# One block schedule for a fused state-space and ReGLU kernel: halved first steps, G moved to the output stage, the C split by one VectorE op

## The chip, the cores and the metric

The kernel runs on one core of a Trainium2 chip. The metric is the device time of one execution in microseconds (us); several executions are timed and the median is given. A profiled execution also has a *span*, from its first to its last instruction; in the profiled runs here the time is 1.6 to 1.8 us longer than the span.

Engines in the profile: PE is TensorE (matmuls), PEld its weight loads, DVE is VectorE, ACT is ScalarE, POOL is GpSimd, SP issues most DMAs. "L442" is a line of that kernel's own source, so the same statement has another number in another kernel.

## The reference

Batch 4, 8 heads, 768 tokens, head size 32, state size 16; then 3072 tokens through a ReGLU feed-forward of 256 to 1536 to 256.

```python
# state-space part, per chunk of tokens (cut)
cum = np.cumsum(log_a, axis=-1)
M = (C @ B.T) * exp(cum_i - cum_j) * causal
y = M @ x + (C @ state) * exp(cum)
state = decay_full * state + sum_j B_j x_j * decay_from_j
# feed-forward
gate = np.maximum(x @ w_gate, 0.0)
val = x @ w_val
out = (gate * val) @ w_out
```

## The kernel before

The kernel works in chunks of 128 tokens. Two chunks are a *pair* (256 tokens, 12 pairs), two pairs are a *block* of the feed-forward (512 tokens, 6 blocks). For a pair, TensorE *turns* B and C (transposes), computes *G* (C times B) into four PSUM banks, the running *state* (A_ps), *inter* (C times state) and *D* (masked G times x). D and inter accumulate in one bank `y`, which is copied to `yT`, the input of the feed-forward. While block b runs, the attention of block b+1 is slipped between its matmuls. ScalarE and VectorE keep to the order of the program even where a later instruction is ready first: in the timeline of block 3 below, a relu whose gate was ready about 100.7 us starts at 102.44, behind a split of C that waited 1.51 us, and VectorE's BT copy, whose turn was done about 100.3, starts at 101.39, behind two others. The kernel uses eight PSUM banks: five are shared by everything (gate, val, G, outputs), and `tp`, `y` and `A_ps` have their own.

The parts that matter here:

```python
def tevac(p, beng, ceng, ceng1=None):       # evacuate a turn: BT, and C split by head parity
    ...
    put(beng, BT, 0, None)                  # inside blocks: beng = VectorE
    for t in range(2):
        put(ceng1 or ceng if t else ceng, CT[:, :, t], 1, t)   # inside blocks: ScalarE, two ops

def gevac(p, q, on_act, meng=None):         # mask one of the four banks of G
    if on_act:
        nc.scalar.copy(out=dst, in_=src)
        (meng or nc.gpsimd).tensor_tensor(out=dst, in0=dst, in1=m, op=ALU.mult)
    else:
        nc.vector.tensor_tensor(out=dst, in0=src, in1=m, op=ALU.mult)

def gv(b, f):                               # one gate/value step, 512 tokens wide, two banks
    g, v = bank("gate"), bank("val")
    ... 2 + 2 matmuls of 512 columns ...
    nc.scalar.activation(r, g, AF.Relu)
    nc.vector.tensor_tensor(out=fst[b][:, f], in0=r, in1=v, op=ALU.mult)   # h

# ... [cut] the prologue does all attention of pairs 0 and 1, then:
for b in range(NBLK):
    for f in range(NF):                     # 12 gate/value steps
        gv(b, f)
        # ... [cut] blocks 0, 1 and 2 on have three different placements.
        # Blocks 0 and 1 hold G and D of a pair here; all hold turns, states, scales.
    fout(b, 0); G(Q); gevacs(Q, ...)        # [cut] blocks 2 on
    fout(b, 1); foevac(b, 1); fout(b, 2)
    G(R); gevacs(R, ...)                    # a pair of the block after next
    Dm(Q); yevac(Q, nc.scalar)
    fout(b, 3); foevac(b, 3)
```

## Time and profile before

| | before |
|---|---|
| median of the three executions | 151.74 us |
| span of the profiled execution | 148.8 us |
| PE / DVE / ACT / POOL busy | 89 / 58 / 53 / 32 % |
| block 0's first gate matmul | 20.1 us |

The busy table of the page gives, per engine, busy us, share of the span and number of instructions:

```profile
PE 131.8 (89%) x1048; PEld 74.8 (50%) x1060; DVE 86.6 (58%) x171; ACT 78.8 (53%) x152; POOL 47.4 (32%) x72
```

TensorE bounds the kernel, but the busy times of its matmuls overlap (379 ns on average for 512 columns, while such matmuls start 216 ns apart), so 89% doesn't say how much is lost. The better measure is the length of each block against its own work. TensorE's timeline gives the first gate matmul of every block; cut there, the windows view of the kernel before reads as follows (stretch, length, then busy us and instructions per engine, granted TensorE clock, DMA share, GB/s). The rows are the prologue, blocks 0 to 5 and the tail:

```profile
0.00:20.12 20.12, 15.68 (x115) 7.74 (x117) 13.43 (x44) 7.20 (x16) 11.96 (x26) 1.00 1.18 170
20.12:45.22 25.10, 22.78 (x198) 13.55 (x199) 14.62 (x27) 13.82 (x30) 9.29 (x13) 1.00 0.73 99
45.22:70.51 25.29, 21.33 (x173) 11.82 (x176) 14.08 (x25) 14.31 (x28) 8.22 (x11) 1.00 0.44 64
70.51:90.63 20.12, 19.23 (x162) 10.94 (x163) 12.76 (x23) 12.07 (x23) 6.89 (x10) 1.00 0.55 79
90.63:110.74 20.11, 19.11 (x160) 10.81 (x161) 12.47 (x22) 12.02 (x23) 6.89 (x10) 1.00 0.56 80
110.74:128.86 18.12, 17.97 (x150) 10.70 (x151) 10.99 (x19) 10.56 (x19) 4.19 (x6) 1.00 0.09 30
128.86:144.66 15.80, 15.71 (x97) 9.24 (x95) 8.26 (x12) 8.24 (x14) 0.00 (x0) 1.00 0.10 34
144.66:148.80 4.14, 0.00 (x0) 0.00 (x0) 0.00 (x0) 0.59 (x1) 0.00 (x0) 0.79 0.18 63
```

A block's feed-forward alone is 48 matmuls of 512 columns, 0.216 us apart, and 48 of 256 columns, 0.109 us apart: 15.6 us. Block 5, which carries nothing else, takes 15.8. Two pairs of attention add about 2.6 us (my estimate, from the distances between their matmuls in the same timeline: 1.3 a pair, itemised in the prediction), so blocks 1 to 4 could take about 18.2 us. Blocks 1, 2 and 3 take 25.3, 20.1 and 20.1.

The waits view of the kernel before (who waited for whom; us in total, times, longest) shows some of it:

```profile
ACT CT L331 <- DVE BT L329: 11.7, 10, 1.5
PE y L410 <- POOL gs L359: 2.6, 4, 0.9
PE o L456 <- DVE h L449: 1.6, 3, 0.8
PE val L445 <- ACT r L448: 1.2, 3, 0.5
```

PE's own entries are small. The largest line is an engine off the critical path, ScalarE, standing still for VectorE before it splits C. How this reaches TensorE is seen in the timeline around one turn in block 3 of the kernel before (start, length, engine, line, op, out<-in, idle before and releaser; rows between those shown are left out):

```profile
99.91 0.40 PE L314 MATMUL tp<-ident,bs 128*128 128x128 bf16 x4
100.14 0.59 PE L442 MATMUL gate<-yT,wg 128*128 128x512 bf16 x2
100.47 0.42 DVE L380 TENSOR_TENSOR Sm<-A_ps,smask 128x256 bf16<-128x256 f32 x1
100.80 0.68 DVE L449 TENSOR_TENSOR h<-r,val 128x512 bf16<-128x512 bf16 x1
101.39 0.28 DVE L329 COPY BT<-tp 128x256 bf16<-128x256 bf16 x1
101.71 0.84 ACT L331 ACTIVATE CT<-tp,tmask 128x256 bf16<-128x256 bf16 x2 [1.51 <-DVE BT L329]
102.44 1.57 ACT L448 ACTIVATE r<-gate 128x512 bf16<-128x512 f32 x3
103.09 0.59 PE L445 MATMUL val<-yT,wv 128*128 128x512 bf16 x2 [0.41 <-ACT r L448]
105.35 0.28 PE L456 MATMUL o<-wo,h 128*128 128x256 bf16 x1 [0.41 <-DVE h L449]
```

The turn is done about 100.3 us. ScalarE's next instruction is the C split, but it waits for VectorE's BT copy, which reads the same `tp`, and that copy stands behind a state copy and an h in VectorE's own queue (from 100.47 to 101.39 us). ScalarE idles 1.51 us, then splits C for 0.84 us, and only then do three relus follow in one burst, the first of which had its gate ready about 100.7 us. The value matmul at 103.09 and the last output matmul at 105.35 pay for it.

### The profile page before, as it was taken

The numbers are of one execution on the slowest core, as the hardware profiler recorded it, in microseconds if no ns is written. First come the engines' busy times: TensorE is split into PE (matmuls) and PEld (weight loads), VectorE is DVE, ScalarE is ACT, GpSimd is POOL, SyncE is SP. The second block draws the span as 40 slices with busy tenths as digits, with TensorE's granted clock in tenths as the row PEclk, the third lists the DMA queues.
The fourth block names the chain that finished last, engine by engine and source line by source line (L and its number), as shares of the span: only waits on it lengthen the run. The fifth ranks groups of instructions, "written<-read, shape, count | busy, mean of one in ns | idle before, by whom it ended". The sixth has DMA issues, their size and how long they took to land. (4 is left out here: it accounts for less than half of the span.)

```text
span 148.8 us, 2882 instructions
## 1 busy us (share of the span) xinstructions
PE 131.8 (89%) x1048; PEld 74.8 (50%) x1060; DVE 86.6 (58%) x171; ACT 78.8 (53%) x152; POOL 47.4 (32%) x72
## 2 busy tenths in 40 slices
PE   6969689977998995779999899998899999999980
PEld 2445335444773443357454476444664447644670
DVE  5369857848154592545666555756738587088500
ACT  3124633676536663446766538766266673467320
POOL 6069530408277055014704038140245003000000
PEclk9999999999999999999999999999999999999997
DMA  4999999994023975002699012995012000120011
GB/s 99 180 162 184 214 202 196 119 119 39 4 73 92 121 98 49 0 0 75 119 105 125 4 44 93 130 121 49 0 71 73 4 0 0 71 75 0 0 71 71
DMA packets 68942, 12.08 MB, mean 81 GB/s; under 512 B 62720, under 2 KB 68928, under 8 KB 68928
## 3 DMA queue, kind: packets, MB, share of 16 engines
q1 hardware_dynamic: 63664, 9.02, 40.2%
q0 software_dynamic: 3184, 2.36, 10.4%
q10 hardware_dynamic: 2080, 0.52, 2.2%
q8 instruction: 8, 0.13, 0.4%
q14 instruction: 6, 0.05, 0.2%
HBM read 11.11 MB, written 3.15 MB: 96 GB/s over the span
## 5 line engine op out<-in xcount | busy, mean ns | idle before, releaser
L449 DVE TENSOR_TENSOR h<-r,val 128x512 bf16<-128x512 bf16 x72 | 48.6, 686 | 34.7 <-ACT r L448 25.8
L448 ACT ACTIVATE r<-gate 128x512 bf16<-128x512 f32 x72 | 41.9, 601 | 11.4 <-PE gate L442 11.2
L442 PE MATMUL gate<-yT,wg 128*128 128x512 bf16 x139 | 42.1, 379 | 1.7 <-DVE yT L422 0.9
L445 PE MATMUL val<-yT,wv 128*128 128x512 bf16 x138 | 41.5, 379 | 1.6 <-ACT r L448 1.2
L456 PE MATMUL o<-wo,h 128*128 128x256 bf16 x288 | 34.8, 273 | 1.6 <-DVE h L449 1.6
L359 POOL TENSOR_TENSOR gs<-gs,maskUT 128x512 bf16<-128x512 bf16 x18 | 20.5, 1155 | 48.8 <-ACT gs L358 36.2
L456 PEld LDWEIGHTS <-h 128*128 128x128 bf16 x288 | 27.3, 98 | 7.9 <-DVE h L449 2.4
L445 PEld LDWEIGHTS <-wv 128*128 128x128 bf16 x144 | 14.0, 97 | 19.4 <-issue 3.2
L331 ACT ACTIVATE CT<-tp,tmask 128x256 bf16<-128x256 bf16 x22 | 9.3, 471 | 18.9 <-DVE BT L329 11.7
L442 PEld LDWEIGHTS <-wg 128*128 128x128 bf16 x144 | 13.0, 97 | 12.0 <-issue 2.3
L260 POOL TENSOR_TENSOR bs<-bcr,scaleBC 128x256 bf16<-128x256 f32 x16 | 9.6, 623 | 16.6 <-DMA bcr<-in_C_dram 11.5
L463 ACT COPY ob<-o 128x512 f32<-128x512 f32 x12 | 7.0, 587 | 8.6 <-PE o L456 8.3
L380 DVE TENSOR_TENSOR Sm<-A_ps,smask 128x256 bf16<-128x256 f32 x20 | 8.4, 418 | 0.6 <-PE A_ps L372 0.5
L159 PE MATMUL w<-warm 128*128 128x512 bf16 x17 | 7.3, 570 | 1.3 <-DVE xr L90 1.2
L428 ACT CAST yT<-y 128x512 bf16<-128x512 f32 x9 | 5.3, 592 | 4.8 <-PE y L410 4.8
L392 PE MATMUL y<-CT,Sm 128*128 128x128 bf16 x40 | 6.2, 220 | 1.4 <-ACT CT L331 0.6
L392 PEld LDWEIGHTS <-Sm 128*128 128x128 bf16 x40 | 3.6, 97 | 6.0 <-issue 1.3
L314 PEld LDWEIGHTS <-bs 128*128 128x128 bf16 x48 | 3.6, 103 | 4.8 <-DVE bs L260 2.0
L314 PE MATMUL tp<-ident,bs 128*128 128x128 bf16 x44 | 4.7, 227 | 1.3 <-DVE bs L260 1.1
L410 PE MATMUL y<-gs,xb 128*32 128x128 bf16 x128 | 3.7, 222 | 1.7 <-POOL gs L359 1.6
L279 POOL CAST xb<-xr 128x512 bf16<-128x512 f32 x8 | 4.9, 612 | 0.0
L260 POOL TENSOR_TENSOR bs<-bcr,wf_422 128x256 bf16<-128x256 f32 x4 | 2.4, 618 | 7.4 <-DVE wf_422 L217 7.4
(167 smaller groups left out, 123.6 us busy)
## 6 DMA issues: line engine op xcount, KB each, us to landing
out_dram<-ob SPq DMA_DIRECT2D x12, 256.0 KB, 2.1
xr<-in_x_dram SPq DMA_DIRECT2D x16, 128.0 KB, 3.6
bcr<-in_B_dram SPq DMA_DIRECT2D x16, 64.0 KB, 3.6
bcr<-in_C_dram SPq DMA_DIRECT2D x16, 64.0 KB, 3.3
wg<-in_moe_w_gate_dram POOLq DMA_DIRECT2D x3, 256.0 KB, 6.3
wv<-in_moe_w_val_dram POOLq DMA_DIRECT2D x3, 256.0 KB, 7.2
wo<-in_moe_w_out_dram POOLq DMA_DIRECT2D x1, 768.0 KB, 9.9
xr<-in_x_dram ACTq DMA_DIRECT2D x2, 256.0 KB, 4.7
```

Of the source, the lines that this page charges most:

```text
L159: nc.tensor.matmul(out=w, lhsT=warm[:, 0:128], rhs=warm, start=True, stop=True)
L260: eng.tensor_tensor(out=bs.rearrange("s k (q t n) -> s k t q n", q=4, t=2)[:, :, t], in0=src[:, :, t], in1=f[:, :, 4 * t:4 * t + 4].to_bro ...
L314: nc.tensor.transpose(out=s["tp"][k][:, i], in_=s["tin"][k][i], identity=ident)
L331: eng.mul(dst, src, tmask[:, t:t + 1])
L359: (meng or nc.gpsimd).tensor_tensor(out=dst, in0=dst, in1=m, op=ALU.mult)
L380: nc.vector.tensor_tensor(out=carry["S"], in0=A_ps, in1=smask, op=ALU.mult)
L392: nc.tensor.matmul(out=s["y"][:, t, i], lhsT=Sm[:, t], rhs=s["CT"][:, i, t], start=not s["open"], stop=False, skip_group_check=True)
L442: nc.tensor.matmul(out=g, lhsT=wg[:, k, fs], rhs=yT[:, k, tk], start=(k == 0), stop=(k == 1))
L445: nc.tensor.matmul(out=v, lhsT=wv[:, k, fs], rhs=yT[:, k, tk], start=(k == 0), stop=(k == 1))
L448: nc.scalar.activation(r, g, AF.Relu)
L449: nc.vector.tensor_tensor(out=fst[b][:, f], in0=r, in1=v, op=ALU.mult)
L456: nc.tensor.matmul(out=o[:, ts % 2], lhsT=fst[b][:, f, ts * 128:(ts + 1) * 128], rhs=wo[:, f], start=(f == 0), stop=(f == NF - 1), skip_gr ...
```

## The change

The intent is one schedule for all blocks:

- The first three gate/value steps of a block (four in block 0) are done in two halves of 256 tokens. The first halves need only the first pair's yT; inter and D of the block's second pair (W) run behind the second first-half (third in block 0), and the second halves come after W's yT copy.
- No G among the gate/value steps. All G stand in the output stage.
- A turn inside a block is evacuated by ScalarE (BT) and VectorE (C, both parities in one op) for the block's first pair P, and by ScalarE alone for its second pair Q (in block 0, Q's turn stands in the output stage and is split like P's). The order in CT becomes parity first.
- G's masks: ScalarE copies 1.5 banks and GpSimd applies `affine_select`; VectorE multiplies 2.5 banks by the mask.
- The prologue starts block 0 after pair 0's yT; pair 1's sort, state, inter and D move into block 0. Two more dummy matmuls keep TensorE busy at the start. The last block's outputs leave in 128-row pieces.

The core of the diff (cut):

```diff
-    put(beng, BT, 0, None)
-    for t in range(2):
-        put(ceng1 or ceng if t else ceng, CT[:, :, t], 1, t)
+    (beng.copy if beng is nc.scalar else beng.tensor_copy)(rows(BT), tokens(0))
+    if ceng is nc.scalar:
+        for t in range(2):
+            nc.scalar.mul(rows(CT[:, t]), tokens(1), tmask[:, t:t + 1])
+        return
+    nc.vector.tensor_tensor(out=out_, in0=src.to_broadcast(shape),
+                            in1=mk.to_broadcast(shape), op=ALU.mult)
 ... [cut] gevac, keep_warm 8 -> 9 and 4 -> 5, prologue, tail
+        nh = 4 if b == 0 else 3
+        for f in range(nh):
+            gvh(b, f, 0)
+            if f == nh - 2:
+                inter(W, 0)
+                inter(W, 1)
+                Dm(W)
+                yevac(W, nc.scalar)
+        for f in range(nh):
+            gvh(b, f, 1)
+        for f in range(nh, NF):
+            gv(b, f)
+            if at("turn P", 8, 6, 5):
+                turn(P)
+                tevac(P, nc.scalar, nc.vector)
+            if at("state P0", 10, 8, 7):
+                state(P, 0)
+            if at("state P1", 11, 10, 9):
+                state(P, 1)
+            if at("turn Q", 99, 9, 8):
+                turn(Q)
+                tevac(Q, nc.scalar, nc.scalar)
+        fout(b, 0)
+        if more:
+            G(P)
+            gevac(P)
+        fout(b, 1)
+        state(Q, 0)
+        fout(b, 2)
+        if more:
+            inter(P, 0); inter(P, 1); Dm(P); yevac(P, nc.scalar)
+            G(Q); gevac(Q); state(Q, 1)
+        fout(b, 3)
```

(Some lines are joined or left out, among them block 0's own. `at(name, x, y, z)` is true after step x in block 0, y in block 1, z in the later blocks.)

More of the change, by code (lines that the diff above doesn't have):

```diff
@@ L123 @@
     nc.vector.memset(warm, 0.0)
+    wide_x(0, nc.scalar, nc.vector)
+    wide_x(1, nc.scalar, nc.vector)
     identf = const.tile([2 * BH, 2 * BH], FP32)
@@ L129 @@
     make_upper_triangular(nc, maskUT[:, 0], 1.0, diag=True)
-    wide_x(0, nc.scalar, nc.vector)
-    wide_x(1, nc.scalar, nc.vector)
     zero1 = const.tile([2 * BH, 1], FP32)
@@ L159, in keep_warm @@
             nc.tensor.matmul(out=w, lhsT=warm[:, 0:128], rhs=warm, start=True, stop=True)
-    keep_warm(8)
+    keep_warm(9)
     wg = glob.tile([128, 2, DF], BF16)
@@ L314, in transp, with tevac @@
             nc.tensor.transpose(out=s["tp"][k][:, i], in_=s["tin"][k][i], identity=ident)
-    def tevac(p, beng, ceng, ceng1=None):
+    def tevac(p, beng, ceng):
         s = st[p]
@@ L321, in tevac, with tokens, rows @@
         s["CT"] = CT = att.tile([128, 2, 2, 128], BF16, tag="CT", name="CT")
-        def put(eng, dst, k, t):
+        wide = p < NWIDE
+        def tokens(k, lead=""):
             src = tp[k]
-            if p < NWIDE:
-                dst = dst.rearrange("s c (m r) -> s c m r", r=2)
-                src = src.rearrange("s r (c m) -> s c m r", c=2)
-            if t is None:
-                (eng.copy if eng is nc.scalar else eng.tensor_copy)(dst, src)
-            elif eng is nc.scalar:
-                eng.mul(dst, src, tmask[:, t:t + 1])
-            else:
-                eng.tensor_scalar_mul(dst, src, tmask[:, t:t + 1])
-        put(beng, BT, 0, None)
-        for t in range(2):
-            put(ceng1 or ceng if t else ceng, CT[:, :, t], 1, t)
+            if wide:
+                return src.rearrange("s r m -> s m r")
+            return src.rearrange("s i m -> s (i m)")
+        def rows(dst):
+            dst = dst.rearrange("s i m -> s (i m)")
+            return dst.rearrange("s (m r) -> s m r", r=2) if wide else dst
+        (beng.copy if beng is nc.scalar else beng.tensor_copy)(rows(BT), tokens(0))
[3 more added lines that the diff above has]
+            return
+        src = tokens(1).unsqueeze(1)
+        out_ = CT.rearrange("s t i m -> s t (i m)")
+        if wide:
+            shape = [128, 2, 128, 2]
+            out_ = out_.rearrange("s t (m r) -> s t m r", r=2)
+            mk = tmask.unsqueeze(2).unsqueeze(3)
+        else:
+            shape = [128, 2, 256]
+            mk = tmask.unsqueeze(2)
+        nc.vector.tensor_tensor(out=out_, in0=src.to_broadcast(shape),
+                                in1=mk.to_broadcast(shape), op=ALU.mult)
     def G(p):
@@ L345, in G @@
                 nc.tensor.matmul(
-                    out=g[q][:, i], lhsT=s["BT"][r, i], rhs=s["CT"][r, i],
+                    out=g[q][:, i], lhsT=s["BT"][r, i], rhs=s["CT"][r, :, i],
                     start=(i == 0), stop=True, tile_position=(32 * q, 0),
@@ L350, in G, with causal, gevac, sevac @@
         s["gs"] = att.tile([128, 4, 4, 128], BF16, tag="gs", name="gs", bufs=2)
-    def gevac(p, q, on_act, meng=None):
+    def causal(dst, n):
+        nc.gpsimd.affine_select(
+            out=dst, in_=dst, pattern=[[0, n], [1, 128]], compare_op=ALU.is_ge,
+            fill=0.0, base=0, channel_multiplier=-1)
+    def gevac(p):
         s = st[p]
-        src = s["gp"][q].rearrange("j i t m -> j (i t) m")
-        dst = s["gs"][:, q]
+        g = [t.rearrange("j i t m -> j (i t) m") for t in s["gp"]]
+        d = s["gs"]
         m = maskUT.to_broadcast([128, 4, 128])
-        if on_act:
-            nc.scalar.copy(out=dst, in_=src)
-            (meng or nc.gpsimd).tensor_tensor(out=dst, in0=dst, in1=m, op=ALU.mult)
-        else:
-            nc.vector.tensor_tensor(out=dst, in0=src, in1=m, op=ALU.mult)
-    carry = {}
+        nc.scalar.copy(out=d[:, 0], in_=g[0])
+        causal(d[:, 0], 4)
+        nc.scalar.copy(out=d[:, 1, 2:4], in_=g[1][:, 2:4])
+        causal(d[:, 1, 2:4], 2)
+        for q in (2, 3):
+            nc.vector.tensor_tensor(out=d[:, q], in0=g[q], in1=m, op=ALU.mult)
+        nc.vector.tensor_tensor(out=d[:, 1, 0:2], in0=g[1][:, 0:2], in1=m[:, 0:2],
+                                op=ALU.mult)
+    S = {}
     def astep(p, i):
         c = 2 * (p % PPB) + i
-        s = st[p]
         if c == NC - 1:
-            carry.pop("S", None)
             return
         nc.tensor.matmul(
-            out=A_ps, lhsT=s["B"][i], rhs=s["x"][i],
+            out=A_ps, lhsT=st[p]["B"][i], rhs=st[p]["x"][i],
             start=(c == 0), stop=(c == NC - 2), skip_group_check=True)
-        carry["next"] = att.tile([128, 2, 128], BF16, tag="Sm", name="Sm")
-    def sevac():
-        if "next" in carry:
-            carry["S"] = carry.pop("next")
-            nc.vector.tensor_tensor(out=carry["S"], in0=A_ps, in1=smask, op=ALU.mult)
-    def inter(p, i):
-        c = 2 * (p % PPB) + i
-        s = st[p]
+    def sevac(p, i):
+        if 2 * (p % PPB) + i == NC - 1:
+            return
+        S[2 * p + i + 1] = n = att.tile([128, 2, 128], BF16, tag="Sm", name="Sm", bufs=5)
+        nc.vector.tensor_tensor(out=n, in0=A_ps, in1=smask, op=ALU.mult)
+    def state(p, i):
+        astep(p, i)
+        sevac(p, i)
+    def y_bank(s):
         if "y" not in s:
@@ L387, in inter @@
             s["open"] = False
-        if c == 0:
+    def inter(p, i):
+        s = st[p]
+        y_bank(s)
+        if 2 * (p % PPB) + i == 0:
             return
-        Sm = carry["S"]
+        Sm = S.pop(2 * p + i)
         for t in range(2):
             nc.tensor.matmul(
-                out=s["y"][:, t, i], lhsT=Sm[:, t], rhs=s["CT"][:, i, t],
+                out=s["y"][:, t, i], lhsT=Sm[:, t], rhs=s["CT"][:, t, i],
                 start=not s["open"], stop=False, skip_group_check=True)
             s["open"] = True
-    def chain(p, i):
-        inter(p, i)
-        astep(p, i)
-        sevac()
     def Dm(p):
         s = st[p]
-        if "y" not in s:
-            s["y"] = mm.tile([128, 2, 2, 128], FP32, tag="y", name="y")
-            s["open"] = False
+        y_bank(s)
         for i in range(2):
@@ L419, in yevac @@
         s = st.pop(p)
-        if eng is None:
-            for t, put in ((0, nc.vector.tensor_copy), (1, nc.scalar.copy)):
-                put(yT[:, t, p * 256:(p + 1) * 256],
-                    s["y"][:, t].rearrange("r i m -> r (i m)"))
-            return
         dst = yT[:, :, p * 256:(p + 1) * 256]
@@ L435, in gv @@
     def gv(b, f):
-        if f == 0:
-            fst[b] = ffn.tile([128, NF, 512], BF16, tag="h", name="h")
         tk = slice(b * 512, (b + 1) * 512)
@@ L449, in gv, with gvh @@
         nc.vector.tensor_tensor(out=fst[b][:, f], in0=r, in1=v, op=ALU.mult)
+    def gvh(b, f, u):
+        if f == 0 and u == 0:
+            fst[b] = ffn.tile([128, NF, 512], BF16, tag="h", name="h")
+        tk = slice(b * 512 + u * 256, b * 512 + (u + 1) * 256)
+        fs = slice(f * 128, (f + 1) * 128)
+        gv_ = bank("gv", (128, 2, 256))
+        for j, w in ((0, wg), (1, wv)):
+            for k in range(2):
+                nc.tensor.matmul(out=gv_[:, j], lhsT=w[:, k, fs], rhs=yT[:, k, tk],
+                                 start=(k == 0), stop=(k == 1), skip_group_check=True)
+        r = ffn.tile([128, 512], BF16, tag="r", name="r", bufs=3)[:, 0:256]
+        nc.scalar.activation(r, gv_[:, 0], AF.Relu)
+        nc.vector.tensor_tensor(out=fst[b][:, f, u * 256:(u + 1) * 256], in0=r,
+                                in1=gv_[:, 1], op=ALU.mult)
     def fout(b, ts):
-        if ts % 2 == 0:
+        if ts % 2 == 0 or b == NBLK - 1:
             fst["o"] = bank("o", (128, 2, DM))
@@ L461, in foevac, with turn @@
     def foevac(b, ts):
+        last = b == NBLK - 1
+        if ts % 2 == 0 and not last:
+            return
         ob = ffn.tile([128, 2, DM], FP32, tag="ob", name="ob", bufs=3)
+        r0 = b * 512 + ts * 128
+        if last:
+            i = ts % 2
+            (nc.vector.tensor_copy if i else nc.scalar.copy)(out=ob[:, i], in_=fst["o"][:, i])
+            (nc.sync if i else nc.scalar).dma_start(out=out[r0:r0 + 128, :], in_=ob[:, i])
+            return
         nc.scalar.copy(out=ob, in_=fst["o"])
-        r0 = b * 512 + (ts - 1) * 128
         nc.sync.dma_start(
-            out=out[r0:r0 + 256, :].rearrange("(i p) m -> p i m", p=128), in_=ob)
-    def gevacs(p, on_act):
-        for q in range(4):
-            gevac(p, q, q in on_act)
+            out=out[r0 - 128:r0 + 128, :].rearrange("(i p) m -> p i m", p=128), in_=ob)
+    def turn(p, apart=False):
+        transp(p, 1, apart)
+        transp(p, 0, apart)
     d0 = wide_decay([0])
     d1 = wide_decay([1])
-    keep_warm(4)
+    keep_warm(5)
     wide_factors([0], d0)
@@ L480 @@
     scale_bc(1, nc.gpsimd)
-    weights(4, 8)
-    transp(0, 1, True)
-    transp(0, 0, True)
-    tevac(0, nc.vector, nc.vector, nc.scalar)
-    sort_wide(0, (nc.scalar, nc.vector), own=True)
-    cast_x(1, nc.scalar)
-    G(0)
-    astep(0, 0)
-    gevac(0, 2, True)
-    weights(8, NF)
+    turn(0, True)
+    tevac(0, nc.scalar, nc.vector)
+    sort_wide(0, (nc.scalar, nc.vector), own=True)
+    G(0)
+    state(0, 0)
+    gevac(0)
+    cast_x(1, nc.gpsimd)
+    weights(4, 8)
+    turn(1, True)
@@ L491 @@
     load(2, nc.sync, nc.sync, nc.sync)
     load(3, nc.sync, nc.sync, nc.sync)
-    gevac(0, 0, False)
-    gevac(0, 1, False)
-    gevac(0, 3, True, nc.vector)
-    sevac()
-    transp(1, 1, True)
-    transp(1, 0, True)
-    tevac(1, nc.scalar, nc.vector, nc.scalar)
-    sort_wide(1)
-    keep_warm(3)
+    tevac(1, nc.scalar, nc.vector)
+    keep_warm(4)
     Dm(0)
     inter(0, 1)
-    astep(0, 1)
-    sevac()
-    yevac(0, None)
-    G(1)
-    gevac(1, 2, True)
+    state(0, 1)
+    yevac(0, nc.scalar)
@@ L509 @@
+    keep_warm(2)
+    G(1)
+    gevac(1)
+    weights(8, NF)
     wait_for(2, 1)
     weights_out(0, NF)
-    gevac(1, 0, False)
-    gevac(1, 1, False)
-    gevac(1, 3, True, nc.vector)
-    inter(1, 0)
-    astep(1, 0)
-    sevac()
-    keep_warm(3)
-    Dm(1)
-    inter(1, 1)
-    astep(1, 1)
-    yevac(1, None)
-    sevac()
     for b in range(NBLK):
-        P, Q, R = 2 * b + 2, 2 * b + 3, 2 * b + 4
-        hasP, hasQ, hasR = P < NPAIR, Q < NPAIR, R < NPAIR
-        for n in (R, R + 1):
+        P, Q, W = 2 * b + 2, 2 * b + 3, 2 * b + 1
+        more = P < NPAIR
+        for n in (P + 2, P + 3):
@@ L529 @@
             if n < NPAIR:
                 load(n, nc.sync, nc.sync, nc.sync)
-        for f in range(NF):
-            gv(b, f)
-            if not hasP:
-                continue
-            if b == 0:
-                if f == 2:
-                    decay()
-                if f == 3:
-                    wide_factors([2, 3], wide_decay([2, 3]))
-                if f == 5:
-                    scale(P, nc.gpsimd, nc.gpsimd)
-                if f == 7:
-                    transp(P, 0)
-                    transp(P, 1)
-                    tevac(P, nc.vector, nc.scalar)
-                if f == 8:
-                    sort_wide(P)
-                if f == 9:
-                    chain(P, 0)
-                    G(P)
-                    gevacs(P, (1, 3))
-                    scale(Q, nc.gpsimd, nc.gpsimd)
-                continue
-            if b != 1 and f == 0:
-                chain(P, 0)
-            if b == 1:
-                if f == 0:
-                    scale(P, nc.gpsimd, nc.gpsimd)
-                if f == 1:
-                    scale(Q, nc.gpsimd, nc.gpsimd)
-                if f == 3:
-                    transp(P, 0)
-                    transp(P, 1)
-                    tevac(P, nc.vector, nc.scalar)
-                if f == 4:
-                    scale(R, nc.gpsimd, nc.gpsimd)
-                if f == 5:
-                    chain(P, 0)
-                    G(P)
-                    gevacs(P, (1, 3))
-                if f == 7:
-                    chain(P, 1)
-                if f == 8:
-                    Dm(P)
-                    yevac(P, nc.scalar)
-                if f == 9:
-                    transp(Q, 0)
-                    transp(Q, 1)
-                    tevac(Q, nc.vector, nc.scalar)
-                if f == 10:
-                    chain(Q, 0)
-                    transp(R, 0)
-                    transp(R, 1)
-                    tevac(R, nc.vector, nc.scalar)
-                if f == 11:
-                    chain(Q, 1)
-                continue
-            if f == 1:
-                scale(Q, nc.gpsimd, nc.gpsimd)
-                if hasR:
-                    scale(R, nc.gpsimd, nc.gpsimd)
-            if f == 2:
-                chain(P, 1)
-            if f == 3:
-                Dm(P)
-                yevac(P, nc.scalar)
-            if f == 5:
-                transp(Q, 0)
-                transp(Q, 1)
-                tevac(Q, nc.vector, nc.scalar)
-            if f == 7:
-                chain(Q, 0)
-            if hasR and f == 8:
-                transp(R, 0)
-                transp(R, 1)
-                tevac(R, nc.vector, nc.scalar)
-            if f == 10:
-                chain(Q, 1)
@@ L609, with at @@
-        if b == 0:
-            chain(P, 1)
+        def at(name, *fs):
+            return more and f == fs[min(b, len(fs) - 1)]
+        nh = 4 if b == 0 else 3
+        for f in range(nh):
+            gvh(b, f, 0)
+            if b == 0 and f == 0:
+                sort_wide(1)
+            if b == 0 and f == 1:
+                state(1, 0)
+            if f == nh - 2:
+                inter(W, 0)
+                inter(W, 1)
+                Dm(W)
+                if b == 0:
+                    state(1, 1)
+                yevac(W, nc.scalar)
@@ new lines @@
+        for f in range(nh):
+            gvh(b, f, 1)
+        for f in range(nh, NF):
+            gv(b, f)
+            if b == 0 and f == 4:
+                decay()
+            if b == 0 and f == 5:
+                wide_factors([2, 3], wide_decay([2, 3]))
+            if at("scale P", 6, 3, 3):
+                scale(P, nc.gpsimd, nc.gpsimd)
+            if at("scale Q", 10, 5, 3):
+                scale(Q, nc.gpsimd, nc.gpsimd)
+            if at("turn P", 8, 6, 5):
+                turn(P)
+                tevac(P, nc.scalar, nc.vector)
+            if b == 0 and f == 9:
+                sort_wide(P)
+            if at("state P0", 10, 8, 7):
[5 more added lines that the diff above has]
+                tevac(Q, nc.scalar, nc.scalar)
@@ L611 @@
+        fout(b, 0)
+        foevac(b, 0)
+        if more:
+            G(P)
+            gevac(P)
+        fout(b, 1)
+        foevac(b, 1)
+        if more:
+            if b == 0:
+                turn(Q)
+                tevac(Q, nc.scalar, nc.vector)
+                sort_wide(Q)
+            state(Q, 0)
+        fout(b, 2)
+        foevac(b, 2)
+        if more:
+            inter(P, 0)
+            inter(P, 1)
             Dm(P)
             yevac(P, nc.scalar)
-            fout(b, 0)
-            transp(Q, 0)
@@ L615 @@
-            transp(Q, 1)
-            tevac(Q, nc.vector, nc.scalar)
-            sort_wide(Q)
-            fout(b, 1)
-            foevac(b, 1)
-            G(Q)
-            gevacs(Q, (1, 3))
-            chain(Q, 0)
-            fout(b, 2)
-            chain(Q, 1)
-            fout(b, 3)
-            Dm(Q)
-            yevac(Q, None)
-            foevac(b, 3)
-            continue
-        fout(b, 0)
-        if hasQ:
-            G(Q)
-            gevacs(Q, (1,))
-        fout(b, 1)
-        foevac(b, 1)
@@ L636 @@
-        fout(b, 2)
-        if hasR:
-            G(R)
-            gevacs(R, (1, 3))
-        if hasQ:
-            Dm(Q)
-            yevac(Q, nc.scalar)
+            G(Q)
+            gevac(Q)
+            state(Q, 1)
         fout(b, 3)
```

## The prediction

> **What bounds the kernel now.** TensorE: its matmuls are busy 131.8 of 148.8 us (the page's busy table), VectorE 58%, ScalarE 53%, GpSimd 32%. Read by FFN block from TensorE's timeline (first gate matmul of each block): block 0 starts at 20.1 us, the others at 45.2, 70.5, 90.6, 110.7 and 128.9; the last matmul ends at 144.6; then 4.2 us of copy and output DMA.
> A block's own FFN work is 15.6 us: 48 gate/value matmuls of 512 columns that start 0.216 us apart and 48 output matmuls 0.109 us apart. Block 5, undisturbed, takes 15.8. A pair's attention work is about 1.3 us (turn 0.22, G 0.33, state 0.22, inter 0.22, D 0.34), 0.66 more for the wide pairs (sort). So blocks 1 to 4 could take about 18.2; they take 25.3, 20.1, 20.1 and 18.1. The excess, mainly blocks 0 and 1, is waiting: in the waits, D for GpSimd's mask multiply 2.6 us (1.16 us each, after a 0.59 us ScalarE copy), an output matmul for the last h 1.6, value matmuls for relu 1.2, the first gate matmul for yT 0.9. ScalarE also waits 11.7 us for VectorE's BT copy before it splits C[...] (about 1.1 us at each of ten turns). Relu queues behind that.
>
> **What the change does.**
> 1. Prologue: block 0 starts once pair 0 has its yT; pair 1's sort, state, inter and D (1.44 us) move behind N=256 halves. I expect the first half at about 15 us, its value matmul held until about 16.4 by the value weights (issued 9.8 us, median landing 7.2). [...] 128-column matmuls start 0.105 us apart until 13.5 us, 0.055 after 14.5[...]. Gain about 4 us, 1.4 of it handed to block 0.
> 2. Halves: four 256-column matmuls per half cost 0.435 us, two halves as much as one full step. ScalarE (0.37 a half) and VectorE (0.42, 0.34 apart) keep up. After D the yT copy (0.59 + 0.1) is covered by one half: about 0.3 us idle per block.
> 3. G leaves gate/value, so its four banks no longer starve gate/value; D has a whole output stage plus two halves (over 2 us) for G's evacuation, so its 2.6 us of waits go. affine_select replaces the 1.16 us GpSimd multiply (my estimate 0.65, from 0.29 for 128 columns and 0.56 against 0.20 for memsets).
> 4. C split: one VectorE op (about 0.69) replaces two of 0.47; ScalarE is rid of it, except for Q.
> 5. Added: D of pair 11 in block 5 (0.56 + 0.3). Tail: half-sized last output, about 0.3 saved.
>
> **Sum.** Block 0 effective from 16, work 21.9 + idle 2.5: ends 40.4. Blocks 1 to 4: 18.2 + 0.9 each: 116.8. Block 5: 16.6: 133.4. Tail 3.9: 137.3; plus 2.9 (time less span, as before): **140.3 us**. Range 136.5 to 145.5. Chances: faster 0.94, same 0.04, slower 0.02.
>
> **What would show it.** First gate matmul near 15 us; block starts about 19 apart from block 1 on; no D wait for GpSimd; one wait of gate for yT (0.2 to 0.4) per block; affine_select well under 1.16 us; TensorE's total matmul work unchanged with its idle time gone.
>
> **What would make it wrong.** Weights landing late in block 0; VectorE overloaded around the output stage (1.7 us of G evacuation plus Sm), so that the halves or the last h wait; Q's turn all on ScalarE delaying the last relus (0.3 to 0.5 a block); slow affine_select; no early full rate.

## The result, and the profile after

The changed kernel takes 138.41 us (138.27 to 139.25, four runs), the one before 151.65 in the runs taken beside it. The ratio is 0.9157, with a 95% interval of 0.9096 to 0.9218. A ratio here is always the mean time of one kernel's fast runs over that of the other's of the same rounds, so it is not quite the ratio of the medians quoted. In e1 the same pair gave 138.9 and 150.71 us, ratio 0.9224. The profiled run (139.25) is the slowest of the fast ones; its TensorE has a granted clock of 0.79 in the prologue and 1.00 after it.

The page's busy table of the changed kernel, and its windows cut at the first halved matmul of each block:

```profile
PE 127.4 (93%) x1130; PEld 81.5 (59%) x1138; DVE 89.4 (65%) x190; ACT 80.5 (58%) x171; POOL 39.1 (28%) x79
```

```profile
0.00:16.37 16.37, 12.75 (x87) 5.60 (x89) 8.52 (x36) 4.77 (x9) 8.43 (x23) 0.79 1.16 161
16.37:41.38 25.01, 23.31 (x230) 15.82 (x229) 17.37 (x35) 15.21 (x35) 8.49 (x15) 1.00 0.96 131
41.38:60.55 19.17, 18.66 (x174) 12.25 (x173) 13.51 (x27) 12.76 (x27) 5.32 (x11) 1.00 0.57 84
60.55:79.58 19.03, 18.79 (x176) 12.37 (x175) 13.32 (x27) 12.76 (x27) 5.55 (x11) 1.00 0.58 84
79.58:98.38 18.80, 18.60 (x176) 12.36 (x175) 12.81 (x26) 12.76 (x27) 5.42 (x11) 1.00 0.58 85
98.38:117.30 18.92, 18.68 (x175) 12.26 (x173) 13.79 (x27) 12.76 (x27) 5.33 (x11) 1.00 0.09 29
117.30:134.10 16.80, 16.57 (x129) 10.87 (x127) 9.63 (x18) 9.44 (x19) 0.60 (x2) 1.00 0.10 33
134.10:137.50 3.40, 0.00 (x0) 0.00 (x0) 0.42 (x1) 0.00 (x0) 0.00 (x0) 1.00 0.21 75
```

Against the rows of before the span loses 3.75 us in the prologue, 0.1 in block 0 (which now also carries pair 1's remainder), 6.1 in block 1, 1.1 and 1.3 in blocks 2 and 3 and 0.7 in the tail; blocks 4 and 5 get 0.8 and 1.0 longer, block 4 because it now turns two pairs and computes two G where it had one (block 1 the other way round: three pairs before, two now), block 5 because D of the last pair now falls into it. The sum is the 11.3 us between the spans. Blocks 1 to 4 now take 18.8 to 19.2.

In the waits view of the changed kernel the wait of ScalarE for BT is gone; what is left of the crossing is VectorE waiting for ScalarE's BT:

```profile
DVE CT L348 <- ACT BT L334: 0.8, 2, 0.6
PE o L484 <- DVE h L461: 0.3, 1, 0.3
```

The timeline around a P turn in block 2 of the changed kernel, to set beside the one above (rows left out):

```profile
66.74 0.39 PE L314 MATMUL tp<-ident,bs 128*128 128x128 bf16 x4
67.16 0.37 ACT L334 COPY BT<-tp 128x256 bf16<-128x256 bf16 x1
67.59 0.60 ACT L460 ACTIVATE r<-gate 128x512 bf16<-128x512 f32 x1
67.74 0.69 DVE L348 TENSOR_TENSOR CT<-tp,tmask 128x512 bf16<-128x512 bf16 x1
```

ScalarE copies BT as soon as the turn is done and goes on with the next relu 0.43 us after it began. VectorE, one step behind by nature (it needs the relu), comes to `tp` when ScalarE has left it.

The head of block 2 in the changed kernel, D and the change from first to second halves (rows left out):

```profile
61.74 0.41 PE L429 MATMUL y<-gs,xb 128*32 128x128 bf16 x16
62.09 0.39 PE L472 MATMUL gv<-yT,wg 128*128 128x256 bf16 x2
62.20 0.59 ACT L442 CAST yT<-y 128x512 bf16<-128x512 f32 x1 [0.19 <-PE y L429]
62.31 0.38 PE L472 MATMUL gv<-yT,wv 128*128 128x256 bf16 x2
62.84 0.38 PE L472 MATMUL gv<-yT,wg 128*128 128x256 bf16 x2
```

Pairs of 256-column matmuls start 0.22 us apart, so the second halves could start at 62.53. They start at 62.84, when the yT copy (until 62.79) is done: 0.31 us are not covered.

### The profile page after: what moved, and what is told of

Read it like the earlier page. It is cut to its first block, busy times and chain, and to the rows that moved or that the text cites. A ratio compares the mean times of both kernels' runs of the same rounds, so it can differ in the third digit from the quotient of the medians.

```text
span 137.5 us, 3080 instructions
## 1 busy us (share of the span) xinstructions
PE 127.4 (93%) x1130; PEld 81.5 (59%) x1138; DVE 89.4 (65%) x190; ACT 80.5 (58%) x171; POOL 39.1 (28%) x79
## 3 DMA queue, kind: packets, MB, share of 16 engines
q0 software_dynamic: 3184, 2.36, 11.9%
## 4 chain that ended last, share of the span: by engine, by line
PE 55%; ACT 2%; DVE 1%; issue 0%; DVEq 0%
PE o L484 19%; PE val L457 12%; PE gate L454 11%; PE gv L472 7%; PE y L429 2%; ACT yT L442 2%; PE y L418 1%; PE A_ps L392 1%; PE tp L314 1%; DVE h L461 0%; DVE ob L497 0%; PE g_1244 L357 0%; PE g_1948 L357 0%; PE g_1639 L357 0%; PE g_993 L357 0%
## 5 line engine op out<-in xcount | busy, mean ns | idle before, releaser
L461 DVE TENSOR_TENSOR h<-r,val 128x512 bf16<-128x512 bf16 x53 | 35.9, 686 | 10.4 <-ACT r L460 9.3
L460 ACT ACTIVATE r<-gate 128x512 bf16<-128x512 f32 x53 | 31.2, 600 | 9.0 <-PE gate L454 7.3
L457 PE MATMUL val<-yT,wv 128*128 128x512 bf16 x106 | 31.5, 379 | 0.4
L365 POOL TENSOR_SCALAR_AFFINE_SELECT gs<-gs 128x512 bf16<-128x512 bf16 (+1 forms) x24 | 11.9, 521 | 64.8 <-ACT gs L376 64.8
L454 PE MATMUL gate<-yT,wg 128*128 128x512 bf16 x99 | 30.0, 379 | 0.0
L476 DVE TENSOR_TENSOR h<-r,gv 128x256 bf16<-128x256 bf16 x38 | 15.8, 421 | 8.0 <-ACT r L475 7.8
L457 PEld LDWEIGHTS <-wv 128*128 128x128 bf16 x106 | 10.4, 98 | 12.6 <-issue 0.2
L475 ACT ACTIVATE r<-gv 128x256 bf16<-128x256 f32 x38 | 14.6, 385 | 3.0 <-PE gv L472 2.2
L472 PE MATMUL gv<-yT,wg 128*128 128x256 bf16 x76 | 14.6, 273 | 0.8
L472 PE MATMUL gv<-yT,wv 128*128 128x256 bf16 x76 | 14.5, 272 | 0.0
L442 ACT CAST yT<-y 128x512 bf16<-128x512 f32 x12 | 7.0, 586 | 11.3 <-PE y L429 8.9
L472 PEld LDWEIGHTS <-wv 128*128 128x128 bf16 x76 | 7.4, 97 | 0.9
```

The costliest lines, as they stand in the source:

```text
L365: nc.gpsimd.affine_select(out=dst, in_=dst, pattern=[[0, n], [1, 128]], compare_op=ALU.is_ge, fill=0.0, base=0, channel_multiplier=-1)
L442: eng.copy(out=dst, in_=src)
L454: nc.tensor.matmul(out=g, lhsT=wg[:, k, fs], rhs=yT[:, k, tk], start=(k == 0), stop=(k == 1))
L457: nc.tensor.matmul(out=v, lhsT=wv[:, k, fs], rhs=yT[:, k, tk], start=(k == 0), stop=(k == 1))
L472: nc.tensor.matmul(out=gv_[:, j], lhsT=w[:, k, fs], rhs=yT[:, k, tk], start=(k == 0), stop=(k == 1), skip_group_check=True)
L475: nc.scalar.activation(r, gv_[:, 0], AF.Relu)
```

## The experiments

Each call took the kernel before on the same chip; its median was 150.58 to 150.79 us. All outputs were correct. Medians of the fast runs, and the ratio of the fast runs to those of the kernel before:

| run | us | ratio | us against e1 |
|---|---|---|---|
| e1 the changed kernel again | 138.9 | 0.9224 | |
| e2 no halves from block 1 on | 142.08 | 0.9446 | +3.2 |
| e3 G of P back among gate/value | 144.19 | 0.9567 | +5.3 |
| e4 one more half, factors late | 138.69 | 0.9204 | -0.2 |
| e5 mask by multiply on GpSimd | 139.24 | 0.9227 | +0.3 |
| e6 C split in two VectorE ops | 139.05 | 0.9234 | +0.15 |
| e7 kernel before, turn engines swapped | 145.44 | 0.9675 | (before: 150.70) |
| e8 one more half, factors early | 137.07 | 0.9107 | -1.8 |
| e9 changed kernel, old turn engines | 146.14 | 0.9687 | +7.2 |
| e10 e8, pair 1 sorted in the prologue | 136.23 | 0.9027 | -2.7 |
| e11 e10, loads of pairs 2, 3 held back | 135.07 | 0.8956 | -3.8 |
| e12 changed kernel, turns all on ScalarE | 139.68 | 0.9284 | +0.8 |

e1 to e4 ran on one chip together, e5 to e8 in a second call, e9 to e11 in a third, e12 in a fourth, each on another chip; "against e1" crosses calls for the last eight, where the before medians differ by up to 0.2 us. One run of e7 and two each of e10 and e11 were slow; with them the medians are 145.96, 136.56 and 135.49; e9's expectation quotes the first (4.7 us gained).

### e1: control

No edit.

> The changed kernel as it is, for control on this chip. About 138.4 us, ratio to the kernel before 0.91 to 0.92. If the time moves by 0.5 us or more between runs with the clock of the first 20 us, the prologue's cold TensorE is a visible part of the scatter.

Measured: 138.9 us (138.5 to 139.61), ratio 0.9224. Its five runs had mean granted clocks from 0.973 to 0.999; the one with 0.999 took 138.5, those with 0.973 and 0.975 took 139.61, 139.31 and 138.9. The scatter of 1.1 us goes roughly with the clock, as expected; in the profiled run all of the clock's loss is in the prologue (0.89 there, 1.00 after).

### e2: halves undone from block 1 on

```diff
-        nh = 4 if b == 0 else 3
+        nh = 4 if b == 0 else 0
+        if b > 0:
+            ... [cut] the tile of h
+            inter(W, 0); inter(W, 1); Dm(W); yevac(W, nc.scalar)
```

> Halves undone from block 1 on: inter, D and the yT copy of pair W stand at the head of the block, and all gate/value steps are full width. Theory (halves hide D's latency): D then waits about 0.5 us for G's evacuation, which now has one output stage (1.3 us) instead of 2.2 us, and the yT copy (0.7 us) is bare where 0.3 us was: 0.9 us per block, five blocks, so about 143 us (+4.5). Rival (moving G out of gate/value is what mattered, the halves are decoration): within 1.5 us of the control, that is below 140.

Measured: 142.08 us, +3.2. The waits of e2 show the bare copy in all five blocks, 0.7 us each, and a first sign of D waiting for G's masks:

```profile
PE gate L454 <- ACT yT L442: 3.4, 5, 0.7
PE gv L472 <- DMA wv<-in_moe_w_val_dram: 1.1, 1, 1.1
PE y L429 <- DVE gs L382: 0.4, 1, 0.4
```

Its D takes 0.66 us on average (0.40 to 1.03 in the five blocks) where the changed kernel's takes 0.41 (timelines). So per block 0.7 + 0.25 us appear and 0.31 go: 0.64, times five is 3.2. I had put 0.9 per block; D's wait was half of what I took it for. The rival is out. The middle line, the value weights, belongs to the start of block 0 and comes up again below.

### e3: G of P back among the gate/value steps

```diff
+            if at("G P", 10, 10, 10):
+                G(P)
+                gevac(P)
         fout(b, 0)
-        if more:
-            G(P)
-            gevac(P)
```

> G of the first pair goes back among the gate/value steps (after step 10), nothing else. Theory (G's four of five banks starve gate/value): TensorE waits 0.8 to 1.2 us more per block in blocks 0 to 4, so 142.5 to 144.5 us. Rival (the stalls of the kernel before came from relu queueing behind the C split, not from banks): under 139.5 us.

Measured: 144.19 us, +5.3; blocks 0 to 4 are 1.0 to 1.1 us longer each. In block 2 of e3:

```profile
73.58 1.01 PE L357 MATMUL g<-CT,BT 32*128 32x256 bf16 x8
75.23 0.38 PE L454 MATMUL gate<-yT,wg 128*128 128x512 bf16 x1 [0.64 <-ACT gs L376]
```

G takes 1.01 us instead of 0.40, and in e3's waits G waits for relus, which empty the banks of gate (0.7 us, 2 times, longest 0.5); the gate after it waits 0.64 us more for ScalarE to empty a bank of G. Bank starvation by G is real and costs about 1.1 us where G stands after step 10, the one place tried. In the kernel before, G stood among the gate/value steps only in blocks 0 and 1.

### e4: one more half, first try

```diff
-        nh = 4 if b == 0 else 3
+        nh = 5 if b == 0 else 4
-            if f == nh - 2:
+            if f == nh - 3:
 ... [cut] decay, factors and scale of block 0 one step later each
```

> One more halved step per block, with D one half earlier relative to the second halves, so that two halves (0.87 us) instead of one (0.435) cover the yT copy. In the changed kernel the second halves start 0.31 us late in each block. Theory (that gap is the yT copy): the gap goes in five or six blocks, minus 1.5 us, about 136.9 us. Rival (D then reaches its waits for G's masks, because it comes one half earlier relative to G, or ScalarE's 0.17 us of extra relu costs as much): within 0.5 us of the control.

Measured: 138.69 us, -0.2: by the total, the rival. But the block lengths of e4 are 25.8, 18.9, 18.7, 18.5, 18.6 and 16.5 us against 25.0, 19.2, 19.0, 18.8, 18.9 and 16.8 of e1. The 0.31 us did go in five blocks, and block 0 gave 0.8 back: the edit had moved pair 2's decay factors one step later, so GpSimd scaled pair 2 later and its turn waited for that (TensorE's waits for GpSimd's scaling rose from 1.8 to 2.6 us). Without the cut by blocks, a gain and a self-made loss would have read as "no effect".

### e5: GpSimd's mask as a multiply again

```diff
-        nc.gpsimd.affine_select(out=dst, in_=dst, pattern=[[0, n], [1, 128]], ...)
+        nc.gpsimd.tensor_tensor(out=dst, in0=dst, in1=maskUT.to_broadcast([128, n, 128]),
+                                op=ALU.mult)
```

> The changed kernel with GpSimd's causal select put back to a multiply by the mask (0.63 us becomes about 1.16 for a full bank). Theory (after the change D has slack): GpSimd's part of G then ends about 0.75 us later, at the end of the slack that the output stage and two halves give (0.58 us in block 2), so D waits 0 to 0.2 us per block: 138.9 to 140 us. Rival (the slow mask multiply was what cost time before): over 141 us.

Measured: 139.24 us, +0.3, within the expectation. The multiply's full bank takes up to 1.16 us, the select 0.64, yet D doesn't wait for either: no such entry is in e5's waits. In the new schedule the faster mask is worth nothing clear of the noise; whether it would have helped the old one, where D waited 2.6 us for the masks, no run shows.

### e6: C split in two VectorE ops

```diff
+        for t in range(2):
+            nc.vector.tensor_scalar_mul(rows(CT[:, t]), tokens(1), tmask[:, t:t + 1])
+        return
```

> The changed kernel with C split by two VectorE ops instead of one; layout and engines as changed. Theory (one op or two is not on the path of TensorE; what counted was taking the split off ScalarE): within 0.4 us of the control (138.9). Rival (VectorE is the tight engine among the gate/value steps): over 140 us.

Measured: 139.05 us, +0.15. That it is one op is worth nothing that can be seen here.

### e7: the kernel before, with only the engines of the turns inside the blocks swapped

```diff
-    put(beng, BT, 0, None)                # VectorE
-    for t in range(2):
-        put(ceng, CT[:, :, t], 1, t)      # ScalarE
+    nc.scalar.copy(dB, sB)                # BT
+    nc.vector.tensor_tensor(out=CT..., in0=src..., in1=tmask..., op=ALU.mult)
 ... [cut] two ops for the wide pairs
```

> The kernel before with only the engines of the turn changed: ScalarE copies BT, VectorE splits C (in one op, two for the wide pairs). One part of the change alone. Theory (relu queues behind ScalarE's two C ops): minus 1 to 2.5 us against 150.7, so 148.2 to 149.7. Rival (G inside gate/value is the whole loss, the split only moves load to the busier VectorE): within 0.5 us of 150.7.

Measured: 145.44 us (five fast runs) against 150.70, ratio 0.9675 (0.9631 to 0.9718). My theory had the sign but half the size: this one part, alone, gives 4.9 us by the ratio. Its blocks take 23.9, 23.5, 19.1, 19.1, 17.9 and 15.8 us; so in blocks 2 and 3 the old schedule, with the swap, is within 0.3 us of the new one (19.03 and 18.80). And the wait of ScalarE for BT, 11.7 us before, is gone from its list.

### e8: one more half, with the factors early

```diff
-        nh = 4 if b == 0 else 3
+        nh = 4
-            if f == nh - 2:
+            if f == (2 if b == 0 else 1):
-            if b == 0 and f == 4:
-                decay()
-            if b == 0 and f == 5:
-                wide_factors([2, 3], wide_decay([2, 3]))
+            if b == 0 and f == 4:
+                wide_factors([2, 3], wide_decay([2, 3]))
+            if b == 0 and f == 5:
+                decay()
 ... [cut] scales of blocks 1 on one step later (Q's in block 1 stays)
```

> The changed kernel with four halved steps in every block, D after the second from block 1 on (so two halves cover the yT copy), block 0 kept, and in block 0 the wide pairs' factors before the other decays. The last try (e4) lost in block 0 what it won in blocks 1 to 5 by starting GpSimd's scaling of pair 2 later. Theory: minus 0.31 us in each of five blocks and minus 0.4 us for the turn of pair 2, so about 137.0 us. Rival (the gap is made good elsewhere): 138.5 us or more.

Measured: 137.07 us, ratio 0.9107: -1.8 us, as expected. Blocks 1 to 5 take 18.9, 18.7, 18.5, 18.6 and 16.5 us.

### e9: the changed kernel with the old engines at the turns

```diff
-                tevac(P, nc.scalar, nc.vector)
+                tevac(P, nc.vector, nc.scalar)
-                tevac(Q, nc.scalar, nc.scalar)
+                tevac(Q, nc.vector, nc.scalar)
```

(and the same for Q's turn in block 0.)

> The changed kernel with the turns inside the blocks evacuated as before the change: VectorE copies BT, ScalarE splits C in two ops. In the old schedule the opposite swap alone (e7) gained 4.7 us. Theory A (relu queues behind the split wherever the turn stands among gate/value steps, so the two parts add up): plus 3 to 5 us, 142 to 144 us. Theory B (the new schedule, with turns spread out and halves at the head, absorbs most of the delay: VectorE and ScalarE have two banks and a half of slack): plus 0 to 1.5 us, below 140.4. In between, the share tells how far the parts overlap.

Measured: 146.14 us, +7.2: more than either theory said. Blocks 1 to 4 take 20.7, 20.5, 20.3 and 20.4 us. The wait of the kernel before is back:

```profile
ACT CT L337 <- DVE BT L334: 11.0, 9, 1.5
PE val L457 <- ACT r L460: 2.2, 4, 0.8
PE o L484 <- DVE h L461: 1.9, 4, 0.7
```

With e1 and e7 this makes a square (medians of the fast runs, in brackets the ratio to the kernel before):

| | old turn engines | new turn engines |
|---|---|---|
| old schedule | 150.70 | 145.44 (0.9675, e7) |
| new schedule | 146.14 (0.9687, e9) | 138.9 (0.9224, e1) |

By the ratios, each part alone gives 4.7 to 4.9 us, and both together give 11.7, that is about 2 more than their sum; the swap is worth 4.9 us in the old schedule and 7.0 in the new one. (The swap covers the turns inside the blocks; the prologue's are as in each schedule.) The new schedule doesn't absorb the crossing; it suffers from it more. The profiles show where: from block 0 to block 4 the swap shortens the old schedule's blocks by 1.2, 1.8, 1.1, 1.0 and 0.2 us (before against e7), the new schedule's by 1.3, 1.5, 1.5, 1.5 and 1.5 (e9 against e1). So 1.3 of the 2 us are in block 4, which turns one pair in the old schedule and two in the new one.

### e10: pair 1 sorted in the prologue

```diff
+    cast_x(1, nc.scalar)                  # early, on ScalarE
-    keep_warm(4)
+    sort_wide(1)
     Dm(0)
 ... [cut] the same two taken out of block 0; the edits of e8
-    keep_warm(2)
+    state(1, 0)
```

> e8 (137.1) with pair 1's sort and first state step in the prologue, in the place of the six dummy matmuls around pair 0's D; ScalarE casts x of pair 1 early. Theory (those dummies are idle TensorE time, and block 0 cannot start before the value weights land at about 16.2 us anyway): block 0 starts no later than 16.9 and is 0.9 to 1.4 us shorter (sort 0.66, state 0.11, the wait of inter for Sm 0.6): 135.7 to 136.3 us. Rival (the dummies keep TensorE at full rate and without them block 0 starts at half rate): 137 us or more.

Measured: 136.23 us (median of the four fast runs, mean 136.18; 136.56 with the two slow ones); ratio of the fast runs 0.9027 against 0.9107 of e8, so 0.9% better, within what the theory expected, if near its upper end. The profile fell into a slow run, whose TensorE is at half rate from 11.95 until about 21 us (256-column matmuls 0.21 us apart, 0.11 afterwards), so its block lengths are not compared. Whether the dummies help is not settled by this: the fast runs scatter about as much as those of e8 (135.51 to 136.75 against 136.94 to 138.0), and only the two slow ones lie further out.

### e11: the loads of pairs 2 and 3 held back

```diff
+        if p >= 2:
+            nc.vector.memset(bcr[0:1, 0, :, 0, 0:1], 0.0)   # the load waits for this
 ... [cut] the loads of x likewise; the edits of e10
-    load(2, ...); load(3, ...)
     tevac(1, nc.scalar, nc.vector)
+    load(2, ...); load(3, ...)
```

> e10 with the loads of pairs 2 and 3 (1 MB) held back until about 13.5 us, so that the first gate and value weights have the DMA engines to themselves. Theory (the first value weights are the floor under block 0's start when the prologue is short): the first value matmul no later than 15.6 us and 0.5 to 1.2 us off e10. Rival (attention's own chain of pair 0, not the weights, sets the start; then holding loads back gains nothing, or costs when pair 2's turn waits for its load): within 0.3 us of e10 or slower.

Measured: 135.07 us (four fast runs, 134.61 to 135.63; 135.49 with the two slow ones), ratio of the fast runs 0.8956 (0.8919 to 0.8993), the fastest version, and 1.1 us off e10 by the ratios, as the theory had it. The clock is not the reason: at a mean granted clock of 0.997 or more e11 took 134.61 to 135.35 us, and e10's one such run 136.36. In its profile, which was fast, the first value matmul comes at 15.34 us, with no wait for a weight:

```profile
15.11 0.39 PE L474 MATMUL gv<-yT,wg 128*128 128x256 bf16 x2
15.34 0.38 PE L474 MATMUL gv<-yT,wv 128*128 128x256 bf16 x2
```

The comparison that shows the floor is with e2 and e12, which were also at full rate (128-column matmuls about 0.06 us apart) from pair 1's turn (11.9 to 12.0 us) on: their first gate matmul comes at 14.71 us, but the value matmul waits 1.1 and 1.2 us for its weights (e2: until 16.18).

### e12: the turns all on ScalarE

```diff
-                tevac(P, nc.scalar, nc.vector)
+                tevac(P, nc.scalar, nc.scalar)
```

(and the same for Q's turn in block 0.)

> The changed kernel with every turn inside the blocks evacuated by ScalarE alone: BT and both halves of C (in e9 VectorE copied BT and ScalarE then split C, which cost 7.2 us). ScalarE has more work here than in e9 (BT comes back to it), VectorE less. Theory W (what costs is that ScalarE, in order, stands still for VectorE's BT, which queues behind an h that needs the relu before it: 11.0 us of such waits in e9): without the crossing the cost nearly goes, 138.9 to 140.2 us. Theory L (ScalarE's load of the split, 0.84 us a turn ahead of the next relu, is what costs): 142 us or more, up to e9's 146.

Measured: 139.68 us, +0.8, where e9 had +7.2. Blocks 1 to 5 are those of the control (19.2, 19.0, 18.8, 18.9, 16.8 us). In the timeline of ScalarE around a P turn in block 2 of e12, the split is still ahead of the relus and costs its 0.85 us, without the idle before it:

```profile
67.37 0.37 ACT L334 COPY BT<-tp 128x256 bf16<-128x256 bf16 x1
67.64 0.85 ACT L337 ACTIVATE CT<-tp,tmask 128x256 bf16<-128x256 bf16 x2
68.37 1.09 ACT L460 ACTIVATE r<-gate 128x512 bf16<-128x512 f32 x2
```

So it is not ScalarE's load. Nor is it VectorE's: in e1 VectorE has the 0.69 us of the C split at every P turn where e9 gives it BT (0.28 us), and e1 is the faster. What costs is that ScalarE stands still for VectorE (11.0 us in e9, no such entry in e12) while VectorE stands in its own queue behind work that needs ScalarE. (The order alone, the same two reads by the same engines in turn, was not run; the swap and e12 both move the work too.) The 0.8 us are in block 0 (26.9 us in e12's profile, which starts it 1.3 us earlier than e1's, 1.2 of it the wait for the value weights, and 1.2 instead of 0.5 us of TensorE waiting for the sorted pair).

## Why the prediction was right, point by point

The time, 138.41 us, lies in the range (136.5 to 145.5), 1.9 us under the 140.3 predicted. The mechanisms held, with one effect left without a size (the C split, below); several terms were mis-sized, and partly cancelled.

- **Start of block 0.** Predicted: first half at about 15 us, value matmul held by its weights until about 16.4. In the profiled run the first half came at 16.37 with no weight wait, since TensorE was at half rate there (128-column matmuls 0.105 us apart from 9.12 us on) and the dummies ahead of D filled 12.4 to 14.2 us. In the runs that were at full rate by 12.0 us (e2, e12) the prediction holds nearly to the letter: 14.71, and the value matmul at 16.18 (e2). Two different causes give the same start; that the sum's 16 us fits the profiled run too is luck.
- **Warm-up.** That two more dummies bring full rate earlier was a guess. The five dummies at 6.0 us ran at full rate (0.25 us each, 0.47 before), but in the profiled run matmuls were at half rate again from 9.12 us, shortly after an idle time of 1.59 us, until between 15.2 and 16.0. Nor do the extra dummies decide it: with the old ones, the same 17 took 7.3 us in the profile of before and 6.2 in that of e7; with the new ones, the five ran at full rate in e1 and e2 (0.25 each) and at half in e11 and e12 (0.46). A gap alone doesn't decide it either: in e1 the rate held over one of 1.95 us before 8.86 and was halved after one of 1.47 at 12.00; in e2 it held over 1.56 and 1.32 us. A gain from the dummies is not shown. And the granted clock is no sure sign: in the trace of before it reads 1.00 from 0 to 13.5 us, where 128-column matmuls started 0.105 us apart, and 1.00 after it, where they started 0.055 apart.
- **Halves.** Predicted 0.3 us idle per block; measured 0.31. Undone from block 1 on they cost 3.2 us (e2); the rest of the gap, 1.5 us over five blocks, could be had too (e8).
- **G out of gate/value.** The mechanism is shown (e3, about 1.1 us a block for one G). In the kernel before it applied to blocks 0 and 1 alone, so it is part of block 1's 6.1 us, with D's waits for the masks (2.6 us before, none after).
- **affine_select.** Estimated 0.65 us, measured 0.64 for 128x512 (0.41 for 128x256), where the multiply by a mask takes 1.16. But in the new schedule its speed isn't on the path (e5).
- **The C split.** This is what the prediction mis-sized. It saw ScalarE's 11.7 us of waiting for BT and that "relu queues behind that", and then gave it no amount of its own: beside it stand only TensorE's listed waits (1.2 us for relu, 1.6 for h). Alone it is worth 4.9 us (e7), in the new schedule 7.0 (e9). And the reason is one engine's wait for the other at `tp`, which both read (11.7 us in the kernel before, 11.0 in e9, no such entry in e7 and e12), not the work (e6, e12). The traces show that the second reader waits, not why it has to. The relus keep their place behind the split: the three that wait there leave in one burst at 102.44 us.
- **Block lengths.** Predicted 19.1 for blocks 1 to 4, measured 19.17, 19.03, 18.80 and 18.92; block 5 predicted 16.6, measured 16.80. The sum was right because it was made from each block's work plus a small idle time, and not from "old time minus named waits", which by my estimate could have accounted for at most 9.2 us (6.3 of waits named, 2.6 at the start, 0.3 at the tail) of the 11.3 by which the span fell.
- **Block 0.** Predicted 24.4 (21.9 of work, 2.5 idle), measured 25.0.
- **Tail.** Predicted 3.9 us, measured 3.4.
- **Time less span.** I added 2.9 us, the median of three runs (151.74) less the span of another run. The profiled run's own time was 150.57 against its span of 148.8, which is 1.8. This alone is 1.1 of the 1.9 us by which the prediction was high.

What stays open: why the crossing costs more in the new schedule than in the old one (7.0 against 4.9 us). Block 4, with two turns for one, holds 1.3 us of it; why blocks 2 and 3, with two turns in both, lose 0.4 to 0.5 us more each, no run here shows. Also open is how much the two extra dummies and the smaller tail pieces are worth by themselves; they were not run alone.

## What to carry to other kernels

Where a trace shows one engine waiting for another because both read the same tile, as ScalarE did for VectorE here (11.7 us), look which comes first: let the engine that is earlier in the dependency chain (here ScalarE, whose relu feeds VectorE) read first and the later one second, or give both reads to one engine; here the crossing the other way cost 4.9 to 7.0 us of 150 while neither of the two was over 65% busy. Judge TensorE by the length of each stage against its own work, from start to start; the waits that the prediction named came to 6.3 us where the span fell by 11.3. And when a change moves nothing, cut it by stage before believing it: a gain of 1.5 us and a self-made loss hid each other in e4, and apart they gave 1.8 us in e8.
